# Attention by head on row halves of TensorE, in two PSUM banks and two token tiles a call

## The chip, the core and the metric

The kernel runs on one core of a Trainium2 chip. The metric is the device time in microseconds (us) of one execution, as the median of several runs. Engines are called PE (TensorE's matmuls), PEld (its weight loads), DVE (VectorE), ACT (ScalarE), POOL (GpSimd) and SP (the engine that issues the DMAs here).

## What is computed

A linear attention without a softmax, then two dense layers, on 4 batches of 576 tokens (2304 tokens) with 8 heads of 64 channels:

```python
kv  = einsum('bhsd,bhse->bhde', k, v)            # per batch and head: 64 x 64
out = einsum('bhsd,bhde->bhse', q, kv)
out = out / sqrt(mean(out * out, -1) + 1e-6) * g_norm
x   = out of all heads, 2304 x 512
x   = ((x @ w_a) * (x @ w_b)) @ w_out            # 512 -> 1536 -> 512
h   = x @ w_in                                   # 512 -> 1024
x   = layernorm(h * softmax(h)) * g_ln @ w_out2  # 1024 -> 512
```

The inputs of the attention are float32; the weights of the two layers are float64 and are decoded on the chip.

## The kernel before, in words

Everything of the two layers runs as three matmuls on split operands: each float32 number is a high part and a low part that TensorE takes in its faster float32 form (`three`, L623). The attention's own matmuls are plain float32, and each shows as two matmul records in the profile.

**Attention.** The heads go in four pairs (NP = 4). `att_kv` (L516) forms the two 64 x 64 products of one pair of heads of one batch: 8 matmuls over four chunks of 128 tokens, then 2 over the last 64 tokens (the tail, whose rows lie on partitions 0 to 63 for an even pair and on 64 to 127 for an odd one). Both heads of a pair write one PSUM bank, head 0 on partitions 0 to 63 and head 1 on 64 to 127. Two ACT copies (L537, L538) put them on the diagonal of a 128 x 128 matrix `bd`, whose other quarters are zero. `att_1` (L546) takes one tile of 128 tokens of a batch (the fifth tile of a batch has 64, so there are 20 tiles): 4 matmuls, one for each pair, with the queries as stationary operand over all 128 rows and `bd` as the moving one (L552), into one PSUM bank. The square (L577, ACT), the sum of it (L579, DVE), a copy of the result out of PSUM (L569, ACT), the bias (L581, ACT), the power -1/2 (L582, POOL) and the product (L583, DVE) follow. `att_2` (L588) transposes the normed tile with 4 PE transposes (L594) into one bank, and ACT (L607) and DVE (L608) write the high and the low part of x. So a tile uses a bank twice, once for L552 and once for L594; the pool `psa` has two banks for all of the attention. The first layer has three tiles of two banks (`psm`), and `psx`, a fourth, is made when the attention has ended.

**First layer.** Tokens go in 6 blocks of 384, the hidden width in 12 slices of 128. `ab_items` (L633) makes both products of a slice and block (24 matmuls of 384 columns, L624 to L626), `y_items` (L687) multiplies with w_out (12 matmuls, L707). A block can start when all its tokens have been through L608 (`tokens_ready`, L613). The second layer comes after the last slice.

**Order.** The order of the instructions is made beforehand by a small planner (`Order`, L45) that has a clock of its own and a cost for every step. While the attention lasts, the main loop (L1004) mixes: each main matmul group gives the attention a credit of twice its cost (L978, L1037), and attention steps run first while there is credit or where no main group is ready (L1024). Among main groups only the first two unfinished slices take part (`next_ab`, L980), the second behind the first. The attention's steps go in a fixed list, `front` (L482): the four pairs of a batch, then its five tiles; the transposes (`back`) come when a tile's product is due. A batch's keys and values wait until the batch two before has been multiplied (L494), since `bd` has two sets. Priorities on ACT, DVE and POOL are ranks: the tile's block for the attention, 1.5 to 5 for the decoding of weights (L273).

**Loads.** SP issues all loads in the order of `a_loads` (L190) with weight chunks between them (`FIRST`, L199). A load waits for a free buffer: 3 for keys and values (512 KB each), 2 tails, 6 for queries, 3 for raw weights (L178).

Of the kernel before, what the change touches and what calls it, by code (L numbers as in the profile page):

```python
# [17 lines left out]
P = 128  # L18
B, H, S, D = 4, 8, 576, 64
NT = B * S  # L20
DM = 512
# [92 lines left out]
def attention_moe_moe_kernel(ctx: ExitStack, tc, kv_in, kv_tail, q_in, g_norm, w1, w_in, w_out2, g_ln, out):  # L114
# [14 lines left out]
    psa = tc.alloc_tile_pool(name="psa", bufs=2, space=bass.MemoryType.PSUM)  # L129
# [3 lines left out]
    w2 = ph2 = psx = None  # L133
# [4 lines left out]
    ps_free = {0: 0.0, 1: 0.0, 2: 0.0}  # L138

    def ps_ready():  # L140
        return min(ps_free.values())

    def ps_tile(nm):
        i = min(ps_free, key=ps_free.get)
        assert ps_free[i] < INF
        ps_free[i] = INF
        pool = psx if i == 3 else psm
        return i, pool.tile([P, 2, 512], F32, tag=f"ps{i}", name=nm)
# [11 lines left out]
    mhalf = cst.tile([P, H], F32, tag="mhalf", name="mhalf")  # L160

    nc.gpsimd.memset(mhalf, -0.5)
    bds = {}
    for b in range(2):
        for p in range(NP):
            t = att.tile([P, P], F32, tag=f"bd{b}_{p}", name=f"bd{b}_{p}", bufs=1)
            nc.vector.memset(t, 0.0)
            bds[b, p] = t
# [9 lines left out]
    R_KV, R_TAIL, R_Q, R_RAW = Ring(3), Ring(2), Ring(6), Ring(3)  # L178
# [24 lines left out]
    def load_one(k):  # L203
        what, x, y = k
        nm = f"{what}{x}_{y}"
        if what == "kv":
            r, t, src, n = R_KV, att.tile([P, 2 * SC * P], F32, tag="kv", name=nm, bufs=3), kv_in[x, y], 4096
        elif what == "tail":
            r, t, src, n = R_TAIL, att.tile([P, 2, 256], F32, tag="tail", name=nm), kv_tail[x], 2048
        elif what == "q":  # L210
            r, t, src, n = R_Q, att.tile([P, S], F32, tag="q", name=nm, bufs=6), q_in[x, y], 2304
# [6 lines left out]
        elif what == "q2":  # L218
            t = arrived["q", x, y][1]
            nc.sync.dma_start(out=t[:, NB:S], in_=q_in[x, y, :, NB:S])  # L220
            arrived[k] = None, t, od.load(4 * (S - NB) * P)
# [258 lines left out]
    NTB = (S + P - 1) // P  # L480
    R_PA, R_X, R_SQ, R_R = Ring(2), Ring(4), Ring(2), Ring(4)
    front = [(w, b, i) for b in range(B) for w, n in (("kv", NP), ("t", NTB)) for i in range(n)]  # L482
    back = []
    bd_ready, x_ready, t_left = {}, {}, {b: NTB for b in range(B)}
    att_left = [B * NTB]
    after_back = [False]

    def front_ready():
        if not front or not R_PA.ok():
            return INF  # L490
        w, b, i = front[0]
        if w == "kv":
            need = [("kv", b, i), ("tail", b, 0)]
            if b >= 2 and t_left[b - 2] or b and not started and not after_back[0]:  # L494
                return INF
        else:
            need = [("q" if b or i < NB // P else "q2", b, p) for p in range(NP)]
            if not (R_X.ok() and R_SQ.ok() and R_R.ok()) or any((b, p) not in bd_ready for p in range(NP)):
                return INF
        if any(n not in arrived for n in need):  # L500
            return INF
        t = max(arrived[n][2] for n in need)
        return t if w == "kv" else max([t] + [bd_ready[b, p] for p in range(NP)])

    def run_front():
        w, b, i = front.pop(0)
        if w == "kv":
            od.pe(0.75, lambda: att_kv(b, i))
        else:
            od.pe(0.88, lambda: att_1(b, i))  # L510

    def run_back():
        _, b, t, x, sx = back.pop(0)
        od.pe(0.5, lambda: att_2(b, t, x, sx))

    def att_kv(b, p):  # L516
        (slot, t, _), tl = arrived.pop(("kv", b, p)), arrived["tail", b, 0][1]
        sp = R_PA.take()
        ps = psa.tile([P, 512], F32, tag="pa", name=f"pkv{b}_{p}")
        r0 = D * (p % 2)  # L520

        for c in range(SC + 1):
            for h in range(2):
                o = ps[h * D:(h + 1) * D, 0:D]
                if c < SC:
                    k, v = (t[:, x * P + h * D:x * P + (h + 1) * D] for x in (c, SC + c))
                else:
                    k, v = (tl[r0:r0 + D, p // 2, x * P + h * D:x * P + (h + 1) * D] for x in range(2))
                nc.tensor.matmul(o, lhsT=k, rhs=v, start=c == 0, stop=c == SC)  # L529
        bd = bds[b % 2, p]  # L530

        def done(t):
            R_PA.give(sp)
            bd_ready[b, p] = t

        od.chain([
            ("A", 0.25, lambda: nc.scalar.copy(out=bd[0:D, 0:D], in_=ps[0:D, 0:D])),  # L537
            ("A", 0.25, lambda: nc.scalar.copy(out=bd[D:P, D:P], in_=ps[D:P, 0:D])),  # L538
            (None, 0, done),
        ], t=od.now + 0.75 + 0.2)  # L540
        R_KV.give(slot)
        if p == NP - 1:
            R_TAIL.give(arrived.pop(("tail", b, 0))[0])
        loads()

    def att_1(b, t):  # L546

        n = min(P, S - t * P)
        sp, sx, ss, sr = (r.take() for r in (R_PA, R_X, R_SQ, R_R))
        ps = psa.tile([P, 512], F32, tag="pa", name=f"o{b}_{t}")  # L550
        for p in range(NP):
            nc.tensor.matmul(  # L552
                ps[0:n, p * P:(p + 1) * P], lhsT=arrived["q", b, p][1][:, t * P:t * P + n], rhs=bds[b % 2, p],
                start=True, stop=True,
            )
        t_left[b] -= 1
        if not t_left[b]:
            for p in range(NP):
                R_Q.give(arrived.pop(("q", b, p))[0])
        loads()  # L560
        x = att.tile([P, H, D], F32, tag="x", name=f"x{b}_{t}", bufs=4)
        sq = att.tile([P, H, D], F32, tag="sq", name=f"sq{b}_{t}")
        r = att.tile([P, H], F32, tag="r", name=f"r{b}_{t}", bufs=4)

        o = ps[0:n].rearrange("t (h d) -> t h d", d=D)
        rank = 1 + (b * S + t * P) // NB

        def copy(when):
            od.chain([("A", 0.48, lambda: nc.scalar.copy(out=x[0:n], in_=o)), (None, 0, lambda t: R_PA.give(sp))],  # L569
                     rank=rank - 0.5, t=when - 0.13)  # L570

        def done(when):
            R_R.give(sr)
            back.append((when, b, t, x, sx))

        od.chain([
            ("A", 0.52, lambda: nc.scalar.activation(out=sq[0:n], in_=o, func=AF.Square, scale=D ** -0.5)),  # L577
            (None, 0, copy),
            ("V", 0.6, lambda: nc.vector.tensor_reduce(out=r[0:n], in_=sq[0:n], axis=AX.X, op=ALU.add)),  # L579
            (None, 0, lambda t: R_SQ.give(ss)),  # L580
            ("A", 0.2, lambda: nc.scalar.activation(out=r[0:n], in_=r[0:n], func=AF.Copy, bias=1e-6)),  # L581
            ("G", 1.75, lambda: nc.gpsimd.tensor_tensor(out=r[0:n], in0=r[0:n], in1=mhalf[0:n], op=ALU.pow)),  # L582
            ("V", 0.8, lambda: nc.vector.tensor_tensor(  # L583
# [562 lines left out]
```

## Time and profile before

| | |
|---|---|
| Median of 3 runs | 720.33 us (720.32 to 720.59) |
| Profiled execution: first to last instruction (span) | 721.4 us |
| PE busy, share of the span, matmul records | 703.8 us, 98%, 4130 |
| PEld busy | 660.6 us, 92% |
| DVE busy | 535.9 us, 74% |
| ACT and POOL busy | 269.9 us, 37%; 255.5 us, 35% |
| Bytes moved by DMA | 61.52 MB, mean 85 GB/s |
| Chain of work that ended last: share of PE | 92% |

For the profiled execution the page gives only its span; it lies 1.1 us above the median of the runs. Busy time is the union of an engine's records. A matmul record is longer than the step to the next one, because matmuls are pipelined: what one costs in a row of them is the distance of their starts.

### The profile page before, as it was taken

What the parts mean: (1) busy time and instruction counts of PE and PEld (TensorE: products, weight loads), DVE (VectorE), ACT (ScalarE), POOL (GpSimd) and SP (SyncE); (2) the same over time, 40 slices, a digit from 0 to 9 for tenths busy, and PEclk for the clock granted to TensorE, in tenths of its full rate; (3) what the DMA queues carried; (4) which work ended last, traced back from release to release, by engine and by line L of the source; (5) the groups of instructions that cost most, each with busy time, mean ns of one, the idle gap of its engine ahead of it and who ended that gap; (6) DMA issues with size and microseconds to landing.
All of it is one profiled execution on the core that took longest, in us unless ns stands there. A gap on an engine that the chain in (4) does not pass through costs nothing.

```text
span 721.4 us, 10647 instructions
## 1 busy us (share of the span) xinstructions
PE 703.8 (98%) x4130; PEld 660.6 (92%) x4130; DVE 535.9 (74%) x801; ACT 269.9 (37%) x515; POOL 255.5 (35%) x245
## 2 busy tenths in 40 slices
PE   5889999999999999999999999999999999999998
PEld 4679999999999999999999999999878888888887
DVE  3898565697989798989898987445597686577560
ACT  4666645233243233333232422112353444444331
POOL 2767224243374336414140504002244252333110
PEclk9999999999999999999999999999999999999999
DMA  8943401032242112142314130023500000000001
GB/s 314 334 144 136 183 1 60 30 118 88 92 171 88 60 59 88 29 146 76 130 60 146 60 117 1 1 88 117 204 1 30 15 30 27 18 16 30 29 30 45
DMA packets 21523, 61.52 MB, mean 85 GB/s; under 512 B 2656, under 2 KB 3936, under 8 KB 21472
## 3 DMA queue, kind: packets, MB, share of 16 engines
q1 hardware_dynamic: 21472, 60.83, 23.4%
q8 instruction: 33, 0.54, 0.3%
q14 instruction: 18, 0.15, 0.1%
HBM read 48.76 MB, written 12.06 MB: 84 GB/s over the span
## 4 chain that ended last, share of the span: by engine, by line
PE 92%; DMA 3%; DVE 3%; ACT 1%; issue 1%; SPq 0%; ACTq 0%; DVEq 0%
PE y L707 21%; PE ab L624 14%; PE ab L625 14%; PE ab L626 14%; PE h L845 10%; PE out L624 5%; PE out L626 5%; PE out L625 5%; PE t L937 2%; PE o L552 2%; DMA kv<-in_kv 1%; PE pkv L529 1%; DMA raw_w<-in_w 1%; PE t L594 1%; DMA tail<-in_kv_tail 1%
## 5 line engine op out<-in xcount | busy, mean ns | idle before, releaser
L624 PE MATMUL ab<-xh,wh_w 128*128 128x384 f32 x576 | 195.1, 339 | 0.0
L625 PE MATMUL ab<-xl,wh_w 128*128 128x384 f32 x576 | 193.1, 335 | 0.3 <-DVE xl L608 0.3
L626 PE MATMUL ab<-xh,wl_w 128*128 128x384 f32 x576 | 193.0, 335 | 0.0
L720 DVE TENSOR_TENSOR ya<-y,ya 128x768 f32<-128x768 f32 x132 | 125.3, 949 | 0.4 <-PE y L707 0.3
L624 PEld LDWEIGHTS ab<-xh,wh_w 128*128 128x128 f32 x576 | 108.6, 189 | 0.9 <-ACT ya L718 0.2
L625 PEld LDWEIGHTS ab<-xl,wh_w 128*128 128x128 f32 x576 | 108.6, 189 | 0.6 <-DVE xl L608 0.6
L626 PEld LDWEIGHTS ab<-xh,wl_w 128*128 128x128 f32 x576 | 108.5, 188 | 0.0
L388 POOL TENSOR_TENSOR f_w<-f_w,wh_w 128x512 f32<-128x512 f32 x36 | 46.9, 1303 | 154.5 <-ACT wh_w L387 139.4
L677 DVE TENSOR_TENSOR ab<-ab,a 128x384 f32<-128x384 f32 x72 | 40.5, 563 | 81.8 <-ACT a L676 76.2
L707 PE MATMUL y<-gh,wh_w 128*128 128x384 f32 x288 | 96.9, 337 | 0.2 <-ACT gh L678 0.2
L707 PE MATMUL y<-gl,wh_w 128*128 128x384 f32 x288 | 96.3, 334 | 0.3 <-DVE gl L679 0.3
L707 PE MATMUL y<-gh,wl_w 128*128 128x384 f32 x288 | 96.2, 334 | 0.0
L676 ACT COPY a<-ab 128x384 f32<-128x384 f32 x72 | 34.4, 478 | 155.5 <-PE ab L626 155.2
L845 PE MATMUL h<-wd,lateh 128*128 128x512 f32 x216 | 58.6, 391 | 0.0
L707 PEld LDWEIGHTS y<-gh,wh_w 128*128 128x128 f32 x288 | 54.1, 188 | 1.1 <-ACT gh L678 0.5
L707 PEld LDWEIGHTS y<-gl,wh_w 128*128 128x128 f32 x288 | 54.1, 188 | 0.5 <-DVE gl L679 0.5
L707 PEld LDWEIGHTS y<-gh,wl_w 128*128 128x128 f32 x288 | 54.1, 188 | 0.0
L389 POOL TENSOR_TENSOR wl_w<-f_w,u_w 128x512 fp32r<-128x512 f32 x36 | 50.2, 1393 | 6.2 <-DVE u_w L309 4.3
L792 POOL TENSOR_TENSOR lateh<-ya,lateh 128x512 fp32r<-128x512 f32 (+1 forms) x18 | 18.0, 1011 | 93.2 <-ACT lateh L791 93.1
L678 ACT CAST gh<-ab 128x384 fp32r<-128x384 f32 x72 | 34.4, 478 | 36.4 <-DVE ab L677 35.9
L845 PEld LDWEIGHTS h<-wd,lateh 128*128 128x128 f32 x216 | 40.3, 188 | 8.4
L845 PE MATMUL h<-latel,lateh 128*128 128x512 f32 x162 | 46.3, 394 | 0.0
(97 smaller groups left out, 1196.3 us busy)
## 6 DMA issues: line engine op xcount, KB each, us to landing
raw_w<-in_w SPq DMA_DIRECT2D x36, 512.0 KB, 3.3
kv<-in_kv SPq DMA_DIRECT2D x16, 512.0 KB, 5.8
out<-ot SPq DMA_DIRECT2D x17, 256.0 KB, 2.0
raw_i<-in_w_in SPq DMA_DIRECT2D x8, 512.0 KB, 3.3
raw_o<-in_w_out SPq DMA_DIRECT2D x8, 512.0 KB, 3.2
so<-raw_o SPq DMA_DIRECT2D x8, 512.0 KB, 2.9
q<-in_q SPq DMA_DIRECT2D x12, 288.0 KB, 6.3
si<-wd SPq DMA_DIRECT2D x6, 512.0 KB, 2.6
```

The lines of the kernel that those rows point to most:

```text
L388: ("G", 1.32, lambda: nc.gpsimd.tensor_tensor(out=f, in0=f, in1=hi.bitcast(F32), op=ALU.subtract)),
L389: ("G", 1.32, lambda: nc.gpsimd.tensor_tensor(out=lo, in0=f, in1=u, op=ALU.add)),
L624: nc.tensor.matmul(o, lhsT=ah, rhs=bh, start=first, stop=False)
L625: nc.tensor.matmul(o, lhsT=ah, rhs=bl, start=False, stop=False)
L626: nc.tensor.matmul(o, lhsT=al, rhs=bh, start=False, stop=last)
L676: ("A", 0.45, lambda: nc.scalar.copy(out=a, in_=ps[:, 0, 0:NB])),
L677: ("V", 0.5, lambda: nc.vector.tensor_tensor(out=g, in0=g, in1=a, op=ALU.mult)),
L678: ("A", 0.45, lambda: nc.scalar.copy(out=gh, in_=g)),
L707: nc.tensor.matmul(o, lhsT=x[:, s], rhs=y, start=f == fs[0] and n == 0, stop=f == fs[-1] and n == 2)
L720: op = ("V", 0.87, lambda: nc.vector.tensor_tensor(out=dst, in0=src, in1=dst, op=ALU.add))
L792: ("G", 2.2 * cost, lambda: nc.gpsimd.tensor_tensor(out=lo[:, n], in0=src, in1=hi[:, n].bitcast(F32), op=ALU.subtract)),
L845: nc.tensor.matmul(o, lhsT=x, rhs=y, start=first and k == m == 0, stop=k == 1 and m == 2, skip_group_check=not first)
```

## The change

Each head becomes a matmul of its own in the second product. The queries of head 0 lie on rows 0 to 63 of TensorE and those of head 1 on rows 64 to 127; both are multiplied with a 64 x 64 matrix (no zero quarters), and head 0 writes one PSUM bank, head 1 the other bank of a two-bank tile. Tokens are cut into 18 tiles of 128 without regard to batches; tiles 4 and 13 hold the end of one batch and the start of the next, and take their queries from a load of their own (`qs`). Five calls of `att_1` and `att_2` take two tiles at once, eight take one. Keys and values go by one pair a call in batch 0, by two in batch 1 and by four in batches 2 and 3, the chunks of all pairs first and then their tails, with one ACT copy a call where 16 calls had two each. Attention and first layer share one pool of four two-bank tiles: before the first main matmul the attention may take any of them, from then on only tile 3, and after the attention the layers have all four. Buffers change: 4 for keys and values, 1 tail, 5 queries; a query buffer holds 512 columns.

```diff
-    psa = tc.alloc_tile_pool(name="psa", bufs=2, space=bass.MemoryType.PSUM)
...
+    ps_free = {n: 0.0 for n in range(4)}
+    def ps_mine(mine=False):
+        if not att_left[0] or mine and not started:
+            return [3, 0, 1, 2]
+        return [3] if mine else [0, 1, 2]
...
-            t = att.tile([P, P], F32, tag=f"bd{b}_{p}", name=f"bd{b}_{p}", bufs=1)
-            nc.vector.memset(t, 0.0)
+    bds = [att.tile([P, NP, D], F32, tag=f"bd{n}", name=f"bd{n}", bufs=1) for n in range(2)]
...
-    R_KV, R_TAIL, R_Q, R_RAW = Ring(3), Ring(2), Ring(6), Ring(3)
+    R_KV, R_TAIL, R_Q, R_RAW = Ring(4), Ring(1), Ring(5), Ring(3)
...
-            a_loads += [kvs[0], ("tail", b, 0)] + kvs[1:] + qs
+            a_loads += [kvs[0], ("tail", b, 0)] + kvs[1:] + [("qs", b - 1, 0)] * (b % 2) + qs
...
+        elif what == "qs":
+            t = att.tile([P, NP, P], F32, tag="qs", name=nm, bufs=1)
+            for c, src in enumerate((q_in[x, :, :, 4 * P:S], q_in[x + 1, :, :, 0:D])):
+                nc.sync.dma_start(out=t[:, :, c * D:(c + 1) * D], in_=src.rearrange("p d t -> d p t"))
...
-    front = [(w, b, i) for b in range(B) for w, n in (("kv", NP), ("t", NTB)) for i in range(n)]
+    front = [("kv", 0, [p]) for p in range(NP)] + [("t", 0, [i]) for i in range(3)]
+    front += [("kv", 1, [0, 1]), ("kv", 1, [2, 3]), ("t", 0, [3]), ("t", 0, [4]), ("t", 0, [5]), ("kv", 2, [0, 1, 2, 3]), ("t", 0, [6, 7]),
+              ("t", 0, [8]), ("t", 0, [9, 10]), ("kv", 3, [0, 1, 2, 3]), ("t", 0, [11, 12]), ("t", 0, [13, 14]),
+              ("t", 0, [15, 16]), ("t", 0, [17])]
...
+        for p in ps_:
+            t = arrived["kv", b, p][1]
+            for c in range(SC):
+                for h in range(2):
+                    k, v = (t[:, x * P + h * D:x * P + (h + 1) * D] for x in (c, SC + c))
+                    nc.tensor.matmul(at(p)[h * D:(h + 1) * D], lhsT=k, rhs=v, start=c == 0 and p - ps_[0] < 2,
+                                     stop=False, skip_group_check=True)
...
-            ("A", 0.25, lambda: nc.scalar.copy(out=bd[0:D, 0:D], in_=ps[0:D, 0:D])),
-            ("A", 0.25, lambda: nc.scalar.copy(out=bd[D:P, D:P], in_=ps[D:P, 0:D])),
+        ops = [("A", 0.2 + 0.05 * len(ps_), lambda: nc.scalar.copy(out=dst, in_=src)), (None, 0, done)]
...
-        for p in range(NP):
-            nc.tensor.matmul(
-                ps[0:n, p * P:(p + 1) * P], lhsT=arrived["q", b, p][1][:, t * P:t * P + n], rhs=bds[b % 2, p],
+                for h in range(2):
+                    hs = slice(h * D, (h + 1) * D)
+                    if len(bs) == 2:
+                        src = arrived["qs", bs[0], 0][1][hs, p, :]
+                    else:
+                        src = arrived["q", bs[0], p][1][hs, off - (S - 4 * P) * (bs[0] % 2):][:, 0:P]
+                    w = P // len(bs)
+                    for m, b in enumerate(bs):
+                        nc.tensor.matmul(
+                            ps[m * w:(m + 1) * w, h, (n * NP + p) * D:(n * NP + p + 1) * D],
+                            lhsT=src[:, m * w:(m + 1) * w], rhs=bds[b % 2][hs, p], start=True, stop=True,
+                        )
...
+            if len(bs) == 1 and (off >= S - P or b % 2 == 0 and off == 3 * P):
+                for p in range(NP):
+                    R_Q.give(arrived.pop(("q", bs[0], p))[0])
...
-            ("G", 1.75, lambda: nc.gpsimd.tensor_tensor(out=r[0:n], in0=r[0:n], in1=mhalf[0:n], op=ALU.pow)),
+            ("G", 1.2 + 0.6 * k, lambda: nc.gpsimd.tensor_tensor(
+                out=r, in0=r, in1=mhalf[:, 0:k * H], op=ALU.pow)),
...
+        for n in range(k):
+            for p in range(NP):
+                nc.tensor.transpose(src[:, p, n * P:(n + 1) * P], x[:, n, p * P:(p + 1) * P], ident)
...
-        b_can = back and back[0][0] <= od.now and R_PA.ok()
+        b_can = back and back[0][0] <= od.now and ps_ready(True) <= od.now
```

## Rows read from the trace of the kernel before

**Rows 1.** Stretches: PE, PEld, DVE, ACT, POOL busy us (records), granted clock, DMA share, GB/s

```profile
0.00:101.70 101.70, 88.89 (x768) 79.04 (x768) 72.71 (x121) 61.60 (x146) 51.56 (x39) 0.97 0.54 197
101.70:512.00 410.30, 410.30 (x2368) 410.30 (x2368) 327.20 (x492) 125.00 (x237) 137.72 (x103) 1.00 0.23 81
512.00:721.40 209.40, 204.59 (x998) 171.22 (x996) 135.94 (x188) 83.25 (x133) 66.25 (x104) 1.00 0.11 38
```

**Rows 2.** The same view, the head in stretches of 10 and 20 us

```profile
0.00:10.00 10.00, 3.73 (x52) 3.12 (x54) 3.82 (x13) 2.90 (x6) 0.73 (x7) 1.00 0.82 305
...
20.00:40.00 20.00, 17.18 (x160) 14.46 (x160) 16.68 (x26) 12.61 (x33) 13.59 (x9) 0.91 0.80 297
40.00:60.00 20.00, 17.82 (x162) 15.23 (x163) 17.18 (x25) 11.42 (x28) 11.82 (x8) 0.91 0.59 217
60.00:80.00 20.00, 20.00 (x174) 18.74 (x173) 16.69 (x30) 15.05 (x36) 11.33 (x7) 1.00 0.24 85
```

**Rows 3.** The same view, short stretches of the first 50 us

```profile
15.00:17.00 2.00, 1.40 (x12) 1.21 (x11) 1.53 (x4) 2.00 (x6) 0.52 (x1) 1.00 0.70 205
17.00:20.00 3.00, 2.29 (x17) 1.70 (x15) 2.82 (x5) 2.76 (x7) 2.98 (x2) 1.00 0.83 284
20.00:24.00 4.00, 2.69 (x32) 2.01 (x32) 3.40 (x6) 3.44 (x9) 1.93 (x2) 1.00 0.82 315
...
30.00:32.00 2.00, 2.00 (x10) 1.90 (x9) 1.38 (x3) 0.41 (x2) 0.28 (x1) 0.50 0.98 394
...
36.00:50.00 14.00, 12.58 (x113) 10.82 (x113) 13.10 (x20) 11.29 (x27) 11.08 (x8) 1.00 0.24 90
```

**Rows 4.** Timeline of PE: start us, duration us, line, operation, form, records

```profile
12.55 3.19 PE L552 MATMUL o<-bd,q 128*128 128x128 f32 x16
...
24.71 0.69 PE L529 MATMUL pkv<-kv 128*64 128x64 f32 x16
...
71.47 1.03 PE L594 MATMUL t<-ident,x 128*128 128x128 f32 x8
...
72.53 0.33 PE L625 MATMUL ab<-xl,wh_w 128*128 128x384 f32 x1
...
74.01 0.69 PE L529 MATMUL pkv<-kv 128*64 128x64 f32 x16
74.62 0.33 PE L529 MATMUL pkv<-tail 64*64 64x64 f32 x4
74.88 0.69 PE L529 MATMUL pkv<-kv 128*64 128x64 f32 x16
...
86.38 1.95 PE L552 MATMUL o<-bd,q 128*128 128x128 f32 x16
...
88.34 0.34 PE L625 MATMUL ab<-xl,wh_w 128*128 128x384 f32 x1
...
90.26 1.09 PE L552 MATMUL o<-bd,q 128*64 128x128 f32 x8
91.28 0.44 PE L707 MATMUL y<-gh,wh_w 128*128 128x384 f32 x1
91.56 0.34 PE L707 MATMUL y<-gl,wh_w 128*128 128x384 f32 x1
```

**Rows 5.** Timeline of PE: last two, and last one, of four 64-row transposes

```profile
81.30 0.28 PE L594 MATMUL t<-ident,x 64*128 64x64 f32 x2
...
81.36 0.22 PE L594 MATMUL t<-ident,x 64*128 64x64 f32 x1
```

**Rows 6.** Groups of ACT and DVE, 0 to 103 us: busy us, mean ns | idle before

```profile
L607 ACT ACTIVATE xh<-t,gn 128x512 fp32r<-128x512 f32 x16 | 10.9, 690 | 7.2 <-PE t L594 7.2
L577 ACT ACTIVATE sq<-o 128x512 f32<-128x512 f32 x16 | 9.7, 608 | 6.0 <-PE o L552 6.0
...
L608 DVE SCALAR_TENSOR_TENSOR xl<-t,gn,xh 128x512 fp32r<-128x512 f32 x16 | 11.8, 747 | 4.1 <-ACT xh L607 4.0
...
L608 DVE SCALAR_TENSOR_TENSOR xl<-t,gn,xh 128x256 fp32r<-128x256 f32 x4 | 1.9, 481 | 2.3 <-ACT xh L607 2.3
```

More of the change, by code (lines that the diff above doesn't have):

```diff
@@ L483, in attention_moe_moe_kernel, with seqs, room, units @@
     back = []
-    bd_ready, x_ready, t_left = {}, {}, {b: NTB for b in range(B)}
-    att_left = [B * NTB]
+    bd_ready, x_ready, b_left = {}, {}, {b: 5 for b in range(B)}
+    kv_ps = {}
     after_back = [False]
+    def seqs(t):
+        return sorted({t * P // S, (t * P + P - 1) // S})
+    def room(r, n):
+        first = r.taken + (r.taken % 2 if n == 2 else 0)
+        return all(i < r.n or i - r.n in r.given or r.taken <= i - r.n < first for i in range(r.taken, first + n))
+    def units(r, n):
+        if n == 2 and r.taken % 2:
+            r.give(r.take())
+        return [r.take() for _ in range(n)]
@@ L507, in run_front @@
         if w == "kv":
-            od.pe(0.75, lambda: att_kv(b, i))
+            od.pe(0.6 * len(i) + 0.3, lambda: att_kv(b, i))
         else:
-            od.pe(0.88, lambda: att_1(b, i))
+            od.pe(0.47 * len(i) + 0.3 + 0.6 * any(len(seqs(x)) == 2 for x in i), lambda: att_1(i))
     def run_back():
[L513 to L522, printed above, removed]
-            for h in range(2):
[L524 to L530, printed above, removed]
-        def done(t):
-            R_PA.give(sp)
-            bd_ready[b, p] = t
-        od.chain([
-            ("A", 0.25, lambda: nc.scalar.copy(out=bd[0:D, 0:D], in_=ps[0:D, 0:D])),
-            ("A", 0.25, lambda: nc.scalar.copy(out=bd[D:P, D:P], in_=ps[D:P, 0:D])),
[L539 to L542, printed above, removed]
@@ L568, in copy @@
         def copy(when):
[L569 removed]
+            od.chain([("A", 0.12 + 0.46 * k, lambda: nc.scalar.copy(out=by_head(x), in_=o)), ps_done(slot)],
                      rank=rank - 0.5, t=when - 0.13)
@@ L573, in done, with sq_read @@
             R_R.give(sr)
-            back.append((when, b, t, x, sx))
+            back.append((when, g, x, ux))
+        def sq_read(t):
+            for u in us:
+                R_SQ.give(u)
+        xa = all_heads(x)
         od.chain([
-            ("A", 0.52, lambda: nc.scalar.activation(out=sq[0:n], in_=o, func=AF.Square, scale=D ** -0.5)),
+            ("A", 0.15 + 0.45 * k,
+             lambda: nc.scalar.activation(out=by_head(sq), in_=o, func=AF.Square, scale=D ** -0.5)),
             (None, 0, copy),
-            ("V", 0.6, lambda: nc.vector.tensor_reduce(out=r[0:n], in_=sq[0:n], axis=AX.X, op=ALU.add)),
@@ L588, in att_2 @@
-    def att_2(b, t, x, sx):
-        n = min(P, S - t * P)
-        sp = R_PA.take()
-        ps = psa.tile([P, 512], F32, tag="pa", name=f"t{b}_{t}")
-        xf = x.rearrange("t h d -> t (h d)")
-        for p in range(NP):
-            nc.tensor.transpose(ps[:, p * P:p * P + n], xf[0:n, p * P:(p + 1) * P], ident[0:n, 0:n])
-        R_X.give(sx)
-        src = ps.rearrange("c (p t) -> c p t", t=P)[:, :, 0:n]
-        tok = b * S + t * P
+            ("V", 0.05 + 0.64 * k, lambda: nc.vector.tensor_reduce(out=r, in_=all_heads(sq), axis=AX.X, op=ALU.add)),
@@ L620, in tokens_ready @@
-        return t
+        return max(x_ready.get(t, INF) for t in range((n + P - 1) // P))
     def three(o, ah, al, bh, bl, first, last):
```

171 lines of the change are left out of this document (107 added, 64 removed).

## The prediction

> **What bounds the kernel now.** I read the stretches first. From 101.7 us, where the last transposes end, to 512 us PE is never idle: 2368 matmuls in 410.3 us, a step of 0.1733 us [rows 1]. That stretch and the second layer behind it (4.8 us idle) do the same work after the change, so the time is decided before 101.7 us. There PE is idle for 101.7 - 88.9 = 12.8 us [rows 1]: 6.3 in the first ten, almost all ahead of the first loads, and 5.0 between 20 and 60 us; from 60 us on there is none [rows 2]. Of the 768 matmuls there 320 form keys by values, 160 are the second product (L552), 80 are transposes; the other 208 belong to the layers and at 0.1733 us take 36.0 us. So 101.7 = 12.8 idle + 36.0 layers + 52.9 for attention, with the drains of TensorE between its forms and with stretches at half clock (30 to 32 us runs at 0.50, that is 1.2 GHz [rows 3]; the mean of the head is 0.97 [rows 1]). The layers' total is fixed, so each us off the 52.9 comes off the end, unless it turns into idle time of PE.
>
> **PE's work, part by part** (prices at full clock, from the timeline [rows 4]).
>
> *Second product.* A full tile costs 0.895: two take from 86.38 to one step before the matmul at 88.34, 1.79. The half tile costs 1.13 by the same measure (90.26 to 91.56). Before: 16 x 0.895 + 4 x 1.13 = 18.8. Afterwards a tile has 16 records of 64 columns, with 64 rows and 128 weight columns, in pairs on two row halves. The trace has no two row halves side by side. Nearest rows: two column halves, whose 16 records start within 0.69 - 0.22 = 0.47 (the last lasts 0.22, like that of [rows 5]), so a pair every 0.06 and two at a time; and 64-row records with 128 weight columns and 64 moving ones, one row half alone, every 0.06 (0.28 - 0.22 [rows 5]). Between them a tile costs 8 x 0.06 = 0.5 if halves overlap, 16 x 0.06 = 1.0 if not. I take 0.5, since column halves show that PE runs two small products at once. But the form changes on entering and leaving: chunks start at 74.01 and last-start at 74.48, the tail at 74.62, so 0.14 for a change, and leaving also exposes the next weight load (a step of 0.28 in place of 0.17), together 0.4 a call. Eight single calls at 0.9 = 7.2, five double ones at 1.4 = 7.0, one more change inside the call with a straddling tile: 14.3. Gain 4.5; a single call gains nothing.
>
> What the two halves do side by side no row here shows; the Trainium skill (TensorE: Matmul & The Clock Gate, "The mechanism") says that weight loads overlap running matmuls where the row groups differ. Its section on LDWEIGHTS speaks against the change: a load takes columns / 1.2 ns whatever its rows, 107 ns for 128 columns, and there will be 16 instead of 8 a tile; in series that is 1.7 us a tile, and the sum would come out near the last rival below. The trace disagrees so far: 64-row loads of 128 columns follow at 0.06 [rows 5].
>
> *Keys by values.* A pair of heads costs 0.875 in a run of calls (74.01 to 74.88), of which 0.47 are chunks and 0.12 the tail; the rest, 0.285, is paid once a call. 16 calls become 8: 14.0 becomes 16 x 0.59 + 8 x 0.285 = 11.7. Another 0.25 is paid at both ends of a run of calls; there were eleven runs, five remain: 1.5. Gain 3.8.
>
> *Transposes.* A tile costs 0.444 (71.47 to 72.53 less a step, over two). Before 16 x 0.444 and four half tiles at about 0.5 (4 x 0.06 and two changes); afterwards 18 x 0.444 = 8.0. Gain 1.1.
>
> PE's work falls by about 9.4, or 10 with fewer exits into the layers.
>
> **What is moved.** Tiles 3 and 4 went to PE between 17 and 22 us, while it waited for the keys of batch 1. They now stand behind that batch's products. Its second pair was multiplied at 24.71 [rows 4], just behind its load, and the loads ahead are nearly the same, so I put the first call at 23.8 to 24.2. Two products take 3.19 us from 12.55 on, where later two take 1.95 [rows 4], so three single ones end near 16; between 16 and 24 PE has only three tiles' transposes, 1.4 us. Idle there: 6.4, against 0.6 + 0.7 + 1.3 = 2.6 between 15 and 24 [rows 3]. That gives back 4 us. The clock then starts low, as it does at 30 us now; I count that as no change.
>
> *Loads.* With four buffers the last keys of batch 1 no longer wait for a multiplication. The three later queries of batch 1 now wait for tile 3 (five buffers), to about 30 us, and land by 35; tile 5 needs them then. The two loads of `qs` are four DMAs of 512 short rows each, on SP ahead of batch 1's and batch 3's queries; nothing needs those before about 32 us, and from 36 to 50 us DMA is busy for 0.24 of the time [rows 3], which hides them.
>
> *ACT, DVE, POOL.* 32 small copies become 8, 20 tiles become 18, fixed costs are shared. They are off the path after 60 us. Before, they end waits of PE; DVE is busy 17.2 of 20 us [rows 2], so relief there helps the weights of slice 1 on time. Booked as nothing; the bounds are 2 us gained, or 2 lost if the order made by the planner fits worse.
>
> **One PSUM tile for all.** From the first main matmul on the attention has tile 3 only. How long is it held (0.2 and 0.3 for the hops between engines are my estimate)? A single product: 0.9 + 0.2 + 0.61 + 0.6 = 2.3 (square and copy are alike [rows 6]); its transposes with high and low part 0.44 + 0.3 + 0.69 + 0.75 = 2.2 [rows 6]. From 0.48 for half and 0.75 for full width [rows 6] double width is 1.28 on DVE, and about 1.1 on ACT; a double product 3.7, its transposes 3.6. Five singles (22.5), five doubles (36.5), four calls of keys by values (11) make 70 us; with 0.25 for the hops of each of 24 turns 76. From 24 us on, the attention ends at 100, as now. Does PE have enough meanwhile? A block of 384 tokens releases 72 matmuls (two slices), 12.5 us. Block 1 takes the tile 19.7 us, to 44; PE has 12.5 + 3.4 + 2.7 + 1.3 = 19.9 for it. Block 2: 16.5 against 18.8. Block 3: 19.5 against 19.8. It just suffices. I book 0.5 us more idle than the 3.7 between 24 and 60 us now.
>
> **The sum.** Against the profiled span of 721.4: -10 + 4 + 0.5 - 0.3 (earlier keys) = -5.8, 715.6. The runs' median lies 1.1 below the span, so 714.5.
>
> **The rivals.**
> - *The waits cost nothing.* PE's idle time in the head stays at 12.8, since layers start earlier and the doubles suit ACT and DVE: -10 to -12, 709. For it: no idle after 60 us and all banks free for the first three tiles. Against: 16 to 24 us has nothing to run. Chance 0.2.
> - *Tile 3 becomes the bound.* Each of its turns takes 1 us longer than I hold, behind a DVE that is 86% busy. Then block 1 comes 8 us late, block 2 costs 2.7, block 3 4.8, block 4 nothing: 15.5 idle instead of 4.2, and 714.5 + 11.3 = 726. Half a us a turn decides between faster and slower. For it: the balance above is even, and before there were two banks. Against: a single tile's uses take only 2.3 and 2.2 by the rows. Chance 0.18.
> - *The row halves do not overlap*, the change doesn't do what it says: 18 x 0.5 = 9 more, 723, less what the early idle time takes up, 722. Against: column halves do. Chance 0.09.
> - *Every weight load goes in turn at the step of a full record*, 0.11 (0.895 / 8): 16 x 0.11 = 1.76 a tile, 18 tiles + 5 of calls = 36.9 against 14.3, 737. Against: the step of 0.06 [rows 5]. Chance 0.03. The Trainium skill's rule on LDWEIGHTS, above, would lead here.
>
> **The numbers.** The forecast, 709 to 719 around 714.5, has 0.5. A range of 707 to 722.5 takes in the first rival, and of the tile's case the milder part; the bounds of ACT and DVE (2 us) are inside. 0.2% is 1.4 us, about what a measurement here can tell from no change. Faster: forecast, first rival and a mild tile, 0.73; within 0.2%: 0.08; slower: tile, no overlap, loads, 0.19.
>
> **What would show it.** Second-product records in pairs every 0.06 us, with about 0.14 before and after a call; 8 copies of ACT for keys by values; PE idle of some 6 us between 16 and 24 us; tile 3 used without pause to about 100 us; no idle of PE after 60 us; the layers' step still 0.1733. Wrong: records every 0.06 in single file; PE waiting for L608 or the copy ahead of each attention call between 30 and 80 us; or layers that start well before 24 us.

## The result: slower, and the profile after

The changed kernel takes 726.86 us (median of 4 runs, 724.68 to 729.03), the kernel before 720.46 us (4 runs, 720.32 to 721.63): a ratio of 1.0079, 95% interval 1.0052 to 1.0105 (the two medians alone give 1.0089). I had forecast 714.5 and put 722.5 as the upper end. In short: the products on row halves cost what the full ones did; the single PSUM tile costs some 3.5 us; and one widened constant moves buffers in SBUF and slows the matmuls of the layers, the second above all, by 2 to 2.5 us, which the prediction did not look at. With these three mended the rest of the idea gives 715.5 us.

First a correction of scale. The profiled execution of after took 724.68 us with a span of 722.9, so 1.8 us lie around a span (1.8 to 1.9 in the runs below, too). The span of 721.4 that the prediction started from is then an execution of some 723.2 us (one run of before with that span, beside experiment 1, took 723.21), one of the longest of the kernel before, and the profile of after shows the shortest of its four. The difference of the two spans, 1.5 us, is therefore much less than that of the medians, 6.4. A second trace with before's instructions (experiment 2) is the better partner for the head. Where the other three runs of after lose another 1.2 to 4.3 us no trace shows.

Stretches of after, as in [rows 1], cut where the last transposes end, then the early ones of [rows 2, 3] (PE, PEld, DVE, ACT, POOL busy us and records, granted clock, DMA share, GB/s):

```profile
0.00:112.05 112.05, 98.42 (x993) 89.20 (x994) 72.57 (x100) 54.14 (x98) 44.95 (x32) 1.00 0.50 179
112.05:512.00 399.95, 399.13 (x2299) 398.38 (x2298) 325.86 (x485) 123.56 (x235) 138.99 (x103) 1.00 0.25 84
512.00:722.90 210.90, 206.03 (x994) 170.49 (x992) 135.69 (x188) 82.58 (x131) 65.67 (x104) 1.00 0.10 38
...
15.00:24.00 9.00, 6.53 (x70) 5.86 (x68) 6.72 (x12) 5.74 (x13) 4.83 (x3) 1.00 0.87 298
20.00:40.00 20.00, 16.19 (x185) 13.38 (x184) 15.81 (x25) 10.14 (x24) 12.24 (x8) 1.00 0.83 294
40.00:60.00 20.00, 18.60 (x199) 16.50 (x199) 17.04 (x23) 10.87 (x20) 14.39 (x10) 1.00 0.34 117
```

The attention now ends at 112.05 instead of 101.7, but 282 matmuls of the layers lie ahead of its last transposes instead of 207, so the end alone says little. I compare what is left of the head, up to the first layer matmul behind these transposes, when the layer matmuls ahead of them are taken off at 0.1733 us each: 112.08 - 48.87 = 63.2 us after, 101.65 - 35.87 = 65.8 in the first trace of before, and 63.25 in the second. No gain shows there, where I had expected 5.8. One trace is a rough measure of it, though: experiments 1 and 5, with the instructions of after in the head, leave 64.9 and 67.5 us.

The timeline of PE after (start us, duration us, line, operation, form, records), against [rows 4]:

```profile
13.19 5.38 PE L618 MATMUL o<-bd,q 64*128 64x64 f32 x48
19.71 1.09 PE L674 MATMUL t<-ident,xbuf 128*128 128x128 f32 x4 [1.14 <-DVE xbuf L663]
...
23.18 1.12 PE L572 MATMUL pkv<-kv 128*64 128x64 f32 x16 [1.33 <-DMA kv<-in_kv]
...
31.44 0.69 PE L618 MATMUL o<-bd,qs 64*64 64x64 f32 x32
...
49.74 0.33 PE L701 MATMUL ab<-xh,wl_w 128*128 128x384 f32 x1
50.00 2.00 PE L618 MATMUL o<-bd,q 64*128 64x64 f32 x32
51.94 0.44 PE L699 MATMUL ab<-xh,wh_w 128*128 128x384 f32 x1
52.22 0.34 PE L700 MATMUL ab<-xl,wh_w 128*128 128x384 f32 x1
...
55.04 0.34 PE L701 MATMUL ab<-xh,wl_w 128*128 128x384 f32 x1
55.31 1.11 PE L618 MATMUL o<-bd,q 64*128 64x64 f32 x16
56.35 0.45 PE L699 MATMUL ab<-xh,wh_w 128*128 128x384 f32 x1
56.63 0.33 PE L700 MATMUL ab<-xl,wh_w 128*128 128x384 f32 x1
```

A double call has 8 pairs more than a single one and lasts 2.00 - 1.11 = 0.89 us longer: 0.111 a pair. The two records of a pair start 6 ns apart, so they do go in pairs; but a pair takes as long as one full record did before (0.895 / 8 = 0.112). With what the call costs the layers around it, a single call is 56.63 - 55.04 less two steps of 0.175, 1.24 us, and a double one 52.22 - 49.74 less the same, 2.13. The straddling tile at 31.44 is the exception: cut into 64 x 64 quarters, its 32 records take 0.69 us altogether.

Two things after the head are new, both against the kernel before. PE waits once in the first layer; these are the rows of PE and of DVE around it:

```profile
208.90 0.34 PE L701 MATMUL ab<-xh,wl_w 128*128 128x384 f32 x1
209.23 0.41 PE L782 MATMUL y<-gh,wh_w 128*128 128x384 f32 x1
210.47 0.44 PE L782 MATMUL y<-gl,wh_w 128*128 128x384 f32 x1 [0.82 <-DVE gl L754]
210.75 0.34 PE L782 MATMUL y<-gh,wl_w 128*128 128x384 f32 x1
```

```profile
199.75 0.69 DVE L311 SCALAR_TENSOR_TENSOR f_w<-raw_w,u_w 128x512 uint32<-128x512 uint32 x1
...
204.66 1.40 DVE L305 TENSOR_SCALAR u_w<-u_w 128x512 uint32<-128x512 uint32 x1
206.09 1.66 DVE L311 SCALAR_TENSOR_TENSOR f_w<-raw_w,u_w 128x512 uint32<-128x512 uint32 x1
207.68 0.55 DVE L752 TENSOR_TENSOR ab<-ab,a 128x384 f32<-128x384 f32 x1
208.14 1.81 DVE L795 TENSOR_TENSOR ya<-y,ya 128x768 f32<-128x768 f32 x2
209.87 0.54 DVE L754 TENSOR_TENSOR gl<-ab,gh 128x384 fp32r<-128x384 f32 x1
```

From 208.90 to 210.75 three steps should take 0.52 us and take 1.85, a loss of 1.3. DVE is late because weight decoding falls just there, with two long steps (L305 and L311, the latter 1.66 against 0.69 at 199.75). The long steps alone are not it: the kernel before has two like them a little earlier, and no such wait.

```profile
204.07 1.40 DVE L305 TENSOR_SCALAR u_w<-f_w 128x512 uint32<-128x512 uint32 x1
205.50 1.67 DVE L309 SCALAR_TENSOR_TENSOR u_w<-raw_w,u_w 128x512 f32<-128x512 uint32 x1
```

What differs is the order on PE: before has products of the layer to run (L624 to L626, 207.34 to past 211) while DVE catches up, and after comes at 209.23 to the group that needs the result of L754.

And the output matmuls of the second layer are slower, of the same form and in the same number (group rows of before, then after; mean ns of one record in the second column behind the bar):

```profile
L625 PE MATMUL out<-wl_o,dh 128*128 128x512 f32 x84 | 32.7, 389 | 0.0
```

```profile
L700 PE MATMUL out<-wl_o,dh 128*128 128x512 f32 x84 | 33.3, 397 | 0.0
```

From start to start the median step is 227 ns before and 231 to 232 after; over the 440 or so steps of these matmuls that is 95.4 against 97.5 us. The first layer's products hardly change (mean step 173.3 and 173.5 ns between 250 and 500 us); over the 2300 or so steps between the attention and the second layer that is another 0.4 us.

### The profile page after: what moved, and what is told of

Same layout as the page of the kernel before. It is cut to its first block, busy times and chain, and to the rows that moved or that the text cites. A ratio compares the mean times of both kernels' runs of the same rounds, so it can differ in the third digit from the quotient of the medians.

```text
span 722.9 us, 10828 instructions
## 1 busy us (share of the span) xinstructions
PE 703.6 (97%) x4282; PEld 658.1 (91%) x4282; DVE 534.1 (74%) x772; ACT 260.3 (36%) x463; POOL 249.6 (35%) x238
## 4 chain that ended last, share of the span: by engine, by line
PE 86%; DVE 10%; issue 1%; DMA 1%; ACT 1%; POOL 0%; SPq 0%; ACTq 0%; DVEq 0%
PE y L782 18%; PE ab L699 12%; PE ab L701 12%; PE ab L700 12%; PE h L920 10%; PE out L699 5%; PE out L700 5%; PE out L701 5%; PE o L618 3%; DVE ya L795 2%; PE t L1012 2%; PE pkv L572 1%; DVE f_w L311 1%; PE t L674 1%; DVE u_w L305 1%
## 5 line engine op out<-in xcount | busy, mean ns | idle before, releaser
L399 POOL TENSOR_TENSOR f_w<-f_w,wh_w 128x512 f32<-128x512 f32 x36 | 48.4, 1345 | 131.1 <-ACT wh_w L398 84.9
L753 ACT CAST gh<-ab 128x384 fp32r<-128x384 f32 x72 | 34.5, 480 | 49.0 <-DVE ab L752 48.4
```

The costliest lines, as they stand in the source:

```text
L399: ("G", 1.32, lambda: nc.gpsimd.tensor_tensor(out=f, in0=f, in1=hi.bitcast(F32), op=ALU.subtract)),
L753: ("A", 0.45, lambda: nc.scalar.copy(out=gh, in_=g)),
```

## The experiments

Ratios are to the kernel before on the same chip, with their 95% interval; "after" is the changed kernel (ratio 1.0079).

**1 and 2: where the buffers lie.** `mhalf`, the operand of the power, grew from 8 to 16 columns, 32 bytes a partition. Everything that is allocated behind it on that side (x, the low parts `late`, the decoded weights `wd`) moves up by 32 bytes; what is allocated from the other side (`dh`, for one) stays. Experiment 1 adds 32 bytes more to after, experiment 2 gives the kernel before the wider tile and uses half of it.

Experiment 1, against after:

```diff
-    mhalf = cst.tile([P, 2 * H], F32, tag="mhalf", name="mhalf")
+    mhalf = cst.tile([P, 3 * H], F32, tag="mhalf", name="mhalf")
```

Experiment 2, against before:

```diff
-    mhalf = cst.tile([P, H], F32, tag="mhalf", name="mhalf")
+    mhalf = cst.tile([P, 2 * H], F32, tag="mhalf", name="mhalf")[:, 0:H]
```

> The changed kernel with the tile of -0.5 widened from 16 to 24 columns, so that x and the buffers of the second layer lie at the same place modulo 64 bytes as in the kernel before (32 instead of 0). Theory 'place': the output matmuls of the second layer took 231 ns a step after the change and 227 before (440 steps, 97.5 against 95.4 us) because of that place; then they go back to 227 and the kernel gains about 2 us, to about 725. Rival 'run': the longer step belongs to the chip or the run and not to the place; then the step and the time (about 727) stay.

> The kernel before with the tile of -0.5 allotted 16 columns and used in 8, so that everything behind it moves by 32 bytes, as in the changed kernel; the instructions are the same. Theory 'place': the step of the output matmuls goes from 227 to 231 ns and the kernel loses about 2 us (722.5, ratio 1.003). Rival 'run': step and time as before (ratio within 0.1% of 1).

Measured: 1 takes 728.42 us, ratio 1.0101 (1.0076 to 1.0125); 2 takes 723.30 us, ratio 1.0035 (1.0023 to 1.0047). The row of experiment 2 beside those above:

```profile
L625 PE MATMUL out<-wl_o,dh 128*128 128x512 f32 x84 | 33.3, 397 | 0.0
```

Experiment 2 has exactly before's instructions, and its row is after's; its first layer has after's mean step, too (173.5 ns). So the place alone makes 2.5 us (1.7 to 3.4), of which the rows show 2.1 + 0.4. Experiment 1 missed: 64 bytes do not bring the step back (229 ns, between the two), so a rule "the same place modulo 64 bytes" falls as I had put it. Its time did not improve: from first to last the output matmuls take 0.7 us less than in after, but the first layer's mean step rises to 173.9 ns, which costs some 0.8.

**3: quarters in place of halves.** Every tile is cut like the straddling one, into 64 x 64 quarters, so that a record has 64 weight columns instead of 128.

```diff
-                    w = P // len(bs)
-                    for m, b in enumerate(bs):
+                    w = D
+                    for m, b in enumerate((bs[0], bs[-1])):
```

> The changed kernel with every token tile of the second product cut into two halves of 64 tokens, as the straddling tiles are: 32 records of 64 weight columns a tile on four quarters of TensorE in place of 16 records of 128 weight columns on two row halves. Theory 'weight load': a pair of row halves takes 0.112 us a step because each record waits for its 128 weight columns, as the full records before did; with 64 columns four records go in 0.058 us, a tile takes 0.47 instead of 0.89, and TensorE's work in the head falls by 16 x 0.42 = 6.7 us; of that 3 to 6 us reach the end (about 722). Rival 'bank': the two row halves hold each other up at their writes into PSUM; then quarters, which write the same two banks, keep about 0.11 a pair, a tile takes 0.9 or more, and the time stays or grows. Third: the tile 3 of PSUM bounds the attention; then the records shorten but the end of the attention and the time stay.

Measured: 721.46 us, ratio 1.0009 (0.9994 to 1.0024). The timeline of PE, a double and a single call:

```profile
49.46 1.16 PE L618 MATMUL o<-bd,q 64*64 64x64 f32 x64
...
53.88 0.69 PE L618 MATMUL o<-bd,q 64*64 64x64 f32 x32
```

Eight more groups of four now take 0.47 us, 0.059 each, half of a pair of halves. Both have the same rows and the same moving columns, so among these products the step goes with the weight columns: 0.111 for 128, 0.059 for 64. That also speaks against the rival of the banks, since quarters write the same two. A rival that I had not named is that the two row halves take turns, at 0.056 a record, near the 0.06 of one row half alone in [rows 5]. The tails of keys by values speak against it: eight records on both row halves take as long (here, in experiment 3) as four on one row half ([rows 4], 74.62: 0.33 us).

```profile
28.64 0.34 PE L579 MATMUL pkv<-tail 64*64 64x64 f32 x8
```

These have 64 weight columns; no run has products with 128 on one row half alone. And the transposes of [rows 5], 128 weight columns at 0.06, do not follow the weight columns; a transpose is one record where a product is two, and no run settles what makes the difference. The second product falls from 19.8 to 11.4 us on PE (each record counted to the start of the next), and 5.4 us of these 8.4 reach the end; PE's idle time between first product and last transposes grows from 8.3 to 13.6.

**4: tile 3 as early as before.** In after, tile 3 goes ahead of batch 1's keys and values again.

```diff
-    front = [("kv", 0, [p]) for p in range(NP)] + [("t", 0, [i]) for i in range(3)]
-    front += [("kv", 1, [0, 1]), ("kv", 1, [2, 3]), ("t", 0, [3]), ("t", 0, [4]), ("t", 0, [5]), ("kv", 2, [0, 1, 2, 3]), ("t", 0, [6, 7]),
+    front = [("kv", 0, [p]) for p in range(NP)] + [("t", 0, [i]) for i in range(4)]
+    front += [("kv", 1, [0, 1]), ("kv", 1, [2, 3]), ("t", 0, [4]), ("t", 0, [5]), ("kv", 2, [0, 1, 2, 3]), ("t", 0, [6, 7]),
```

> The changed kernel with token tile 3 of the attention put back ahead of batch 1's keys and values in the order, where TensorE waits for them. Theory 'moved work': the idle time between 15 and 24 us takes up its 1.3 us and the queries of batch 1 are free to load earlier, so the 0.34 us wait for a query at 35.6 us goes too: 1 to 2 us less. Rival: the attention is held by its PSUM tile after 30 us, and the time stays within 0.5 us.

Measured: 726.27 us, ratio 1.0075 (1.0057 to 1.0093), no gain. The waits only go to other places (2.4 us at 34.5, 1.2 at 42.4, 1.0 at 50.1). So the postponed tile was not what made after slow.

**5 and 6: after with its buffers at the old place.** The narrow `mhalf` comes back, and the wide one lies in the pool that is released after the attention; 5 is after, 6 is experiment 3 with this.

```diff
-    mhalf = cst.tile([P, 2 * H], F32, tag="mhalf", name="mhalf")
+    mhalf = cst.tile([P, H], F32, tag="mhalf", name="mhalf")
+    mhalf2 = att.tile([P, 2 * H], F32, tag="mhalf2", name="mhalf2", bufs=1)
+    nc.gpsimd.memset(mhalf2, -0.5)
...
-                out=r, in0=r, in1=mhalf[:, 0:k * H], op=ALU.pow)),
+                out=r, in0=r, in1=mhalf2[:, 0:k * H], op=ALU.pow)),
```

> The changed kernel with the 16-column tile of -0.5 for the attention put into the attention's own pool and the 8-column one left where it was, so that x and the second layer's buffers lie at exactly the addresses of the kernel before (17120 instead of 17152 for the first). Theory 'relative place': moving these buffers by 32 bytes against the ones on the other side of the memory (weights and transposed rows, which did not move) lengthens the output matmuls' step (227 to 231 ns, 229 at 64 bytes); then the step is 227 again, the second layer 2.1 us shorter, and the median 2 to 3 us below that of the changed kernel (726.9): 724. Rival: the longer step came with another order of PSUM tiles in the changed kernel too; then the step stays at 231 here.

> Quarters of TensorE for all tiles of the second product, and the old addresses. If both act as alone and add up: 721.5 - 2.1 to 2.8 = 719 (ratio 0.998), the first version below the kernel before. If the gain of the quarters (5.4 us) was already waiting time that another limit takes back, 720.5 or more.

Measured: 5 takes 724.04 us, ratio 1.0050 (1.0032 to 1.0068), with the step back at 227 ns; 6 takes 720.72 us, ratio 1.0003 (0.9988 to 1.0018), also at 227 ns. The group row of 5:

```profile
L702 PE MATMUL out<-wl_o,dh 128*128 128x512 f32 x87 | 33.9, 389 | 0.0
```

That is 2.8 us off after (2.1 by the ratios), though the intervals overlap; on the quarters only 0.4 to 0.7 shows, where the step promises 2. The profiled execution of 6 has 1.0 us more idle time in the head than that of 3 (behind the first product), which would take half of it; the rest is inside the intervals. The step is settled by the rows (every kernel of this study at the old place has 227 ns, every one 32 bytes up 231 to 232), the time less sharply.

**7: a second PSUM tile.** The attention may take one of the layers' three tiles while two of them are free.

```diff
+        if mine and sum(ps_free[n] <= od.now for n in range(3)) >= 2:
+            return [3, 0, 1, 2]
         return [3] if mine else [0, 1, 2]
```

> The changed kernel in which the attention may take any PSUM tile whenever at least two of the layers' three are free. Theory 'tile 3': the waits of transposes for the low part of x (1.6 us at 38 us, 0.7 at 45.7) and the late end of the attention (112 against 99 to 101.5 us) come from the single tile; then the attention ends near 101 us, waits of PE between 35 and 50 us fall from 3.3 us to about 1.5 and the median falls by 1 to 2 us (725). Rival 'chain': the waits are for DVE, which is behind whatever the tiles are; then PE's idle time in the head stays at 8 us and the median within 0.7 us of 726.9, or layers that wait for a tile make it longer.

Measured: 722.96 us, ratio 1.0031 (1.0018 to 1.0043), 3.5 us (0.48%) less than after. Stretches of the head and of 205 to 215 us in experiment 7:

```profile
0.00:100.34 100.34, 86.72 (x932) 79.07 (x933) 70.28 (x94) 50.93 (x92) 46.41 (x32) 1.00 0.56 200
```

```profile
205.00:215.00 10.00, 10.00 (x60) 10.00 (x59) 7.19 (x9) 4.06 (x9) 9.03 (x7) 1.00 0.25 97
```

The attention ends at 100 us again with 219 layer matmuls ahead of it, and the wait at 210 us is gone; it is in after and in experiments 1 and 3 to 6, all with one tile, and in none with two. So part of the tile's price (1.3 us) falls due 100 us after the attention. I read it so: the late attention moves later weight decoding into a stretch where DVE is needed (busy 9.04 us of 205 to 215 in after, 7.19 here). That is not shown by itself: the planner's order differs, too, and in experiment 8 DVE is busy 9.77 us there without a wait. The head itself gives 1.0 us (62.2 against 63.2 over the layers' own time), less than traces of one order differ by. Neither theory describes this. PE's idle time between first product and last transposes stays at 8.3 us and that from 35 to 50 us at 3.4, as 'chain' had it, and yet the time falls, by more than 'tile 3' had forecast. What the experiment prices is the order that comes of a second tile, not waits for a tile.

**8 and 9: all three, and all but the quarters.** 8 is after with the quarters of 3, the place of 5 and the tile of 7; 9 is 8 with after's row halves.

> Quarters, old addresses and borrowed tiles together. If all three act: 717 to 718 (ratio 0.996). If the borrowed tiles change nothing: as with quarters and addresses alone (719). If they hold up the layers: above that.

> The changed kernel with the second tile for the attention and the buffers back in their place, but with the row halves of 128 weight columns left as the change has them. If the three losses are independent, it comes to 726.9 - 2.8 - 3.9 = 720.2, no different from the kernel before, and the quarters alone make the 4.7 us to 715.5: then the products on row halves, as the change has them, are worth nothing on their own. If the row halves do save what the prediction booked and only the waits and the place hid it, it comes to 716 or less, near the version with quarters. Second-product records in pairs every 0.112 us, output matmuls at 227 ns, no wait of PE at 210 us.

Measured: 8 takes 715.50 us, ratio 0.9937 (0.9914 to 0.9960), the fastest kernel of the study. 9 takes 721.79 us (717.66 to 723.59 in 12 runs), ratio 0.9990 (0.9973 to 1.0007). So the losses nearly add up (726.9 - 2.8 - 3.9 - 5.4 = 714.8 by the medians; by the ratios 0.9932, measured 0.9937), and with place and tile mended the change as it was made cannot be told from the kernel before. Stretches of experiment 8:

```profile
0.00:96.47 96.47, 79.18 (x1188) 72.10 (x1189) 69.33 (x94) 50.46 (x92) 46.23 (x33) 0.93 0.61 208
96.47:512.00 415.53, 415.04 (x2389) 413.89 (x2388) 332.03 (x498) 129.39 (x244) 142.17 (x106) 1.00 0.25 86
```

Of its head 58.35 us are not the layers' own, against 63.25 to 65.8 before, though it idles more between products (11.9 us against 7.4).

**10, 11 and 12: the order in experiment 8.** 10 takes keys and values of batches 1 to 3 by one pair a call; 11 puts tile 3 ahead of batch 1's; 12 takes batch 1's in one call.

The first line of the list in 8, then in 10, 11 and 12 (in 10 the calls of batch 3 in the next line are split alike):

```python
    front += [("kv", 1, [0, 1]), ("kv", 1, [2, 3]), ("t", 0, [3]), ("t", 0, [4]), ("t", 0, [5]), ("kv", 2, [0, 1, 2, 3]), ("t", 0, [6, 7]),
    front += [*[("kv", 1, [p]) for p in range(NP)], ("t", 0, [3]), ("t", 0, [4]), ("t", 0, [5]), *[("kv", 2, [p]) for p in range(NP)], ("t", 0, [6, 7]),
    front += [("t", 0, [3]), ("kv", 1, [0, 1]), ("kv", 1, [2, 3]), ("t", 0, [4]), ("t", 0, [5]), ("kv", 2, [0, 1, 2, 3]), ("t", 0, [6, 7]),
    front += [("kv", 1, [0, 1, 2, 3]), ("t", 0, [3]), ("t", 0, [4]), ("t", 0, [5]), ("kv", 2, [0, 1, 2, 3]), ("t", 0, [6, 7]),
```

> The version with quarters, place and second tile, but keys and values by one pair of heads a call in all four batches (16 calls where that version has 8). My price of a call is 0.285 us on PE, so 8 more calls cost 2.3 us, and 717.8 if nothing else moves; if runs of calls split up as well, up to 3.8, 719.3. Rival: the calls' cost lies in time in which PE waits in the head anyway (11.9 us idle there), or the earlier start of a batch's products gives it back: 715.5 within 1 us, and the grouping of keys and values is worth nothing.

> The version with quarters, place and second tile, and tile 3 multiplied and transposed before the keys and values of batch 1, as in the kernel before. That version waits 3.0 us of PE at 15.5 and 2.0 us at 20.8 with nothing to run. If these waits cost the end their length, tile 3 (0.5 us of product and 0.44 of transposes, with a wait for its square and its power in between) fills about 1 us of them, and block 1 starts earlier by as much: 714.5 or, with less waiting for tile 3 later on, 713.5. Rival, as the earlier try with one tile showed: the wait only moves to behind batch 1, where the tile is missing: 715.5 within 1 us.

> The version with quarters, place and second tile, and batch 1's keys and values in one call of four pairs instead of two of two. On PE that saves one call, 0.285 us. It also waits for the last of the four loads before the first product, some 4 us later than now, in a stretch where PE has nothing else: then the waiting before the call grows by up to 2 us and the end with it, 717.5. Rival: splitting by pairs costs 7 to 8 us against calls of four (723.7 against 715.5), so larger calls pay beyond the price on PE, and this one gives 1 us or more: 714.5 or less.

Measured: 10 takes 723.70 us, ratio 1.0039 (1.0024 to 1.0053); 11 takes 721.66, ratio 1.0013 (1.0003 to 1.0024); 12 takes 716.37, ratio 0.9933 (0.9917 to 0.9948), not to be told from 8: neither the loss of 2 us nor the gain of 1 that stood against each other came out. Both theories for 10 and 11 missed: 7 us and 5.5 us lost where at most 3.8 was expected, or a gain. Experiment 11 shows where; its waits of PE, POOL's rows ahead of the wait, and a stretch of 10 us on either side of 50:

```profile
PE t L678 <- DVE xbuf L667: 4.8, 1, 4.8
```

```profile
50.23 3.15 POOL L665 TENSOR_TENSOR r<-r,mhalf 128x16 f32<-128x16 f32 x1 [7.55 <-DVE f_w L315]
```

```profile
40.00:50.00 10.00, 10.00 (x169) 9.34 (x169) 8.01 (x12) 4.91 (x8) 1.38 (x2) 0.74 0.17 55
50.00:60.00 10.00, 5.16 (x111) 4.40 (x110) 7.02 (x7) 3.96 (x9) 9.77 (x5) 0.83 0.78 270
```

In 10 and 11 the planner puts only 180 layer matmuls ahead of the last transposes, in 8 and 12 it puts 219. At 51 us PE has then nothing left, and stands 4.8 us (in 10: 4.2) for the first double tile, whose power on POOL alone takes 3.15 us; and the granted clock is 0.74 and 0.83 around it, that is, partly at 1.2 GHz, where 8 has 1.00 from 40 us on. So these two runs do not price a call or a tile; as I read them, they price an order in which PE's supply runs out. Why the planner drops 39 matmuls there I did not follow up.

## Why the prediction was wrong

*"Between them a tile costs 8 x 0.06 = 0.5 if halves overlap, 16 x 0.06 = 1.0 if not. I take 0.5."* This is the step that failed first: the price of a pair of row halves, 0.06 in the sum, measured 0.111. The halves go in pairs, and a tile takes 8 x 0.111 = 0.89, as if they did not overlap at all: the rival *The row halves do not overlap* has 16 x 0.06 = 1.0 for it, nearer than the 0.5 of the sum, if not for its reason (experiment 3). My two nearest rows each shared one trait with the new record and lacked another: the column halves had 64 weight columns, the 64-row transposes stood alone. Neither was a bound, and the full record's own step, 0.112, was the nearer row: same number of weight columns, and the same number of steps once two records go together. With 1.24 us a single call and 2.13 a double one, 13 calls come to about 20 us, measured 19.8, against the 14.3 that I booked and the 20.2 of the kernel before. The booked prices, 0.9 and 1.4, are those of quarters: by the same measure 0.82 and 1.29 in experiment 3.

That the step of these products goes with the weight columns is what experiment 3 shows. The Trainium skill (TensorE: Matmul & The Clock Gate, "LDWEIGHTS (loading the stationary operand)") has a load take its columns / 1.2 ns whatever its rows: by an estimate from that rule 107 ns for 128 columns and 53 for 64, near the 111 and 59 here. I cited that rule and set it aside because of the 64-row transposes, which it still does not give; the measured steps agree with it once a pair of halves, or four quarters, counts as one load, and not with loads in file as in my last rival (1.76 us a tile, measured 0.89). The Trainium skill (TensorEngine Tiling (Array Packing), "Theoretical Speedup") gives up to 2 where a dimension, here the contraction, has 64 or less; with 128 weight columns and 64 moving ones the measured gain is none (0.89 us a tile against 0.895), and with quarters it is 1.9 (0.47).

*Keys by values, -3.8; transposes, -1.1.* From 17.8 to 15.8 us and from 9.65 to 9.5 in the two profiles: half of the first is seen, the second not. The rest went where I put no price. In after the first three tiles' products take 5.38 us at 13.19, 0.224 a pair, and transposes and keys up to 29 us also take nearly twice their later time (1.09 for transposes, against 0.60 at 37.64; 1.12 for keys, against 0.69 in [rows 4]); in the kernel before they have their full step from 16 to 27 us.

The granted clock of that stretch reads 1.00 in both. But these are the durations that the same forms have at a granted clock of 0.50 (1.2 GHz), as experiment 3 shows them: a stretch, keys and the transposes of two tiles in it, and such transposes later, at 1.00.

```profile
20.00:25.00 5.00, 2.31 (x41) 1.89 (x37) 4.51 (x5) 1.06 (x3) 4.50 (x4) 0.50 1.02 359
...
23.47 1.12 PE L572 MATMUL pkv<-kv 128*64 128x64 f32 x16 [2.69 <-DMA kv<-in_kv]
...
24.95 1.97 PE L674 MATMUL t<-ident,xbuf 128*128 128x128 f32 x8
...
59.37 1.03 PE L674 MATMUL t<-ident,xbuf 128*128 128x128 f32 x8
```

And the clock entries that the trace keeps begin only at 29.7 us in after, at 15.0 and 15.6 in the two traces of before; ahead of the first entry the view prints 1.00 (the first keys, at 5.38, take 1.12 under it in before and after alike). So I take after to run at 1.2 GHz up to 29.7 us, twice as long as before. The six kernels with row halves (after, 1, 4, 5, 7 and 9) have their first entry at 27.6 to 37.7 us, five of the six with quarters at 14.4 to 15.2 us, experiment 11 at 28.2. Ahead of it the full products run in before from 12.55 us on, the row halves in after from 13.19; that these raise the clock later is not shown by itself. *"The clock then starts low, as it does at 30 us now; I count that as no change"* put this at nothing. Behind the keys' arrival at 23.18, where PE hardly waits any more, the slow records cost some 2.5 us, an estimate from the rows: 0.4 for the first keys there, 1.0 for the transposes of two tiles, 1.1 for the other keys and the tails.

*"That gives back 4 us."* Between 15 and 24 us PE idles 2.5 us, as before, and not the 6.4 that I forecast: the slow records fill the hole. Experiment 4 agrees that the postponed tile lost nothing there.

*"It just suffices."* The single tile does not suffice: the attention ends at 112, not 100, and a second tile gives 3.5 us. I had named it as a rival at 726 with a chance of 0.18. That the time came out there is luck, for its reason did not: I expected 11 us more idle time, and the trace has 3.4 us from 30 to 80 us and no wait over 1.6 us there. The price is mostly elsewhere, the wait at 210 us for one.

*"That stretch and the second layer behind it do the same work after the change, so the time is decided before 101.7 us."* The same work, but not at the same speed: 2.1 us in the step of the output matmuls, 0.4 in that of the first layer, 1.3 in the wait. I costed every edit on the engines and none of the allocation; the diff's most harmless line, `mhalf` twice as wide, was worth over a third of the loss.

*"The runs' median lies 1.1 below the span."* Beside experiment 1 the times of before lie from 720.1 to 723.2, and 1.8 us around its span put the profiled one at the top of that. The offset should have been taken as unknown, by some 2 us.

Right was PE's idle time from 60 to 112 us (0.2 us), and nearly right were the loads: the first call of batch 1's keys, which I put at 23.8 to 24.2, starts its first pair at 20.7 and its second at 23.18, just behind that pair's transfer. With the second product near its booked price and the other two losses mended, experiment 8 comes to 715.5, near the 714.5 of the sum; as several terms differ, that is in part luck and no proof of each.

## What to carry to other kernels

Splitting a float32 matmul by rows saved nothing here, with 128 weight columns kept and 64 moving ones; split the columns too, and check the price on the nearest row that has the same number of weight columns. Treat every changed tile size as a move of all tiles behind it, and compare the step of untouched matmuls in the two traces before anything else. Read the clock from the durations of one form, too, where the view may have no entry yet. When a resource is taken from one stage, look for its price where that stage's delayed side work lands, not only at the resource.

## What was not expected of the hardware

Moving the buffers of one side of SBUF by 32 bytes against those of the other changes the step of 128 x 512 matmuls from 227 to 231 or 232 ns, by 64 bytes to 229; the 384-column products of the first layer hardly change (173.3 to 173.5 ns, and 173.9 at 64 bytes). The runs show that it is the place, not why. A four-way cut into quarters starts four records every 59 ns, two row halves two every 111 ns.
